# Fused attention, mixture of experts and gated layer: experts in two groups of four, and a fixed table of operations in place of the planner

## The chip, the cores and the metric

The kernel runs on one core of a Trainium2 chip. The metric is the device time of one execution in microseconds (us); lower is better. Three runs of the kernel before gave 447.46, 447.50 and 449.27 us, median 447.5.

## What is computed

Three layers follow one another on 1536 tokens (batch 2, 768 positions) of width 512. First, attention with 8 heads of 64, in which every query and every key is given to the nearest of 16 centroids of its head, and a query sees only keys of the same centroid. Second, a soft mixture of 8 experts with 4 slots each:

```python
logits = x @ phi                                   # 1536 x 32
d = softmax of logits over the tokens; c = softmax of logits over the slots
slot_input = (d.T @ x).reshape(8, 4, 512)
for e in range(8):
    h = np.maximum(slot_input[e] @ w1[e], 0.0)     # 4 x 1024
    slot_out[e] = h @ w2[e]                        # 4 x 512
x = c @ slot_out
```

Third, a root-mean-square norm and `(silu(xn @ w_gate) * (xn @ w_val)) @ w_out`, with 1536 inner columns. All arrays are float32.

## The kernel before, in words

**Attention.** The heads are taken in eight pairs. `prepare(i)` loads and transposes pair i (`turn`, `keep`), splits queries and keys in a high and a low part (`head`, `rest`), scores them against the centroids (`cluster`), makes one-hot rows (`argmax`, `onehot`, `ok`, `oq`) and moves parts with SyncE DMAs. Each pair has two units (halves of the queries). `unit(u)` computes scores once for the row maxima (`s1`, line 617, and `s1max` on VectorE, line 629), again with keys on the partitions (`s2`, lines 697 and 699), exponentiates on ScalarE (`exp`, line 706), multiplies with the values (`av`, line 723), and sums the six exponentials of the unit (`acc`, line 305, five additions of 128x768). The PSUM ring `big` has three buffers for `turn`, `s1`, `s2` and `lT`.

**Experts.** The slot inputs (`SITz`) are ready some 8 us after attention's last matmul. The 64 weight tiles of 512 KB (w1 and w2, 32 each) are loaded in the order in which the loop of `tile_kernel` at line 1997 lists them, the first 40 while attention runs, the rest as buffers come free. Experts go in four pairs. For a pair, `h1` (line 1454) accumulates over four parts of the width, with two experts times two halves of the 1024 inner columns in the four 32-row strips of one bank; then `relu`, four transposes (`hT`, line 1468), a copy (`hTe`), four `h2` (line 1480), a copy (`h2e`), and `cols` (line 1495, 8 matmul records), which adds the two halves with the matrix `F8` and writes the slot outputs by columns; `socs` and `gcols` copy them with and without the norm's gain. `warm` operations are matmuls without use that fill TensorE's waits; W1, W2, W3 and W9 are their numbers in the last pair.

**Gates.** `gram` and `cq` give the norm from the slot outputs, `x2`, `rms` and `scale` finish it, `part` and `cT` put the scaled slot weights in place, `gp` and `put` multiply the slot outputs with the gate and value weights. After that TensorE does 72 `mm` (line 1810) and 144 `om` (line 1848, three matmuls each) until the end. Weights of the last layer are decoded on ScalarE and VectorE (`mag`, `bits`) and split by `hi` and `lo`; `lo` and some of the `hl` run on GpSimd (line 305).

**Order.** Each operation is a closure with the engines that may run it, estimated durations, a key, and what it depends on; `Sched.op` collects some 1,900 of them, numbered from 0 in order of creation. `Sched.run` (line 201) plans them at build time: it takes again and again the ready operation and engine with the earliest start after penalties (keys with the offsets KO by name and SHIFT by number) and emits it. The order of emission is the order on each engine; waits between engines are semaphores that the framework adds.

Of the kernel before, what the change touches and what calls it, by code (L numbers as in the profile page):

```python
# [27 lines left out]
def bc(ap, n):  # L28
# [23 lines left out]
W9 = 8  # L52
# [4 lines left out]
W1 = 16  # L57
W2 = 8
W3 = 9
# [27 lines left out]
KO = {  # L87
    "acc": 1106.61, "argmax": 340.28, "av": 1317.56, "bits": 77.89, "both": -631.52, "cT": -252.33, "cTe": 2148.93,
    "centroids_": -906.44, "cevac": -692.62, "cluster": 703.68, "clusterT": -435.04, "cols": -526.12,
    "cq": -1953.73, "csm": -1921.26, "dexp": 1823.66, "drec": -318.51, "ds": -3013.83, "dsum": 256.8, "dz": 1821.6,  # L90
    "exp": 552.16, "fes": -661.41, "fexp": -316.11, "fold": -1112.56, "four": -693.77, "fsi": 2185.37,
    "fz": -548.31, "gcols": -2661.57, "gh": 2566.76, "gp": -1829.04, "gpk": 615.23, "gram": -328.99, "h1": -2309.88,
    "h2": 1318.49, "h2e": -2012.01, "hT": -343.76, "hTe": -479.39, "head": 3947.79, "hf": -705.62, "hh": -47.09,
    "hi": -212.93, "high": -1707.34, "hl": 524.04, "keep": 2847.0, "lT": 3.15, "lga": -820.49, "lgm": 934.58,
    "lgt": 814.78, "lgx": -617.39, "lgx0": -2320.67, "linv": -192.64, "lo": 333.83, "load": -352.41,
    "low": -2417.19, "lsum": 2484.96, "mag": 1056.41, "mb": 1281.87, "mbe": 155.41, "mm": 857.14, "mp": 4.41,
    "mp1": -354.58, "mpT": 217.04, "mrow": -453.01, "mv": -459.26, "mx": 1177.33, "nmT": -1237.86, "nrow": 431.94,
    "oT": -1122.62, "od": 1854.19, "oe": -269.77, "ok": -155.6, "om": 1947.6, "onehot": -2302.02, "oq": 996.66,
    "osb": 2866.99, "part": 1651.97, "pre": -2523.99, "put": -52.28, "put4": 2025.22, "qhi": -32.32, "qlo": 2773.53,
    "raw": -660.15, "ready": -508.02, "relu": -165.55, "rest": -573.48, "rms": 1037.95, "root": -316.14,  # L100
    "rowmm": 460.36, "rowput": -750.84, "s1": -1.39, "s1max": -454.29, "s2": 0.21, "scale": 1161.73, "sel": -868.48,
    "setup": 363.79, "si": 91.62, "siT": -250.83, "siT0": 277.65, "siTe": 414.23, "side": 336.02, "sie": 105.19,
    "silu": 2.05, "siz": -1847.17, "socs": 527.72, "square": -516.11, "sums": 484.54, "to_out": 2146.21,
    "to_tail": 3598.45, "to_wp": -1357.1, "to_wv": -909.45, "to_wx": -442.15, "to_wy": 771.46, "to_wz": 3452.96,
    "trans": -76.76, "turn": -5.08, "warm": 109.11, "wload": 2775.16, "x2": -540.95, "xrow": 1179.62,
}


# [5 lines left out]
class Op:  # L114
    __slots__ = ("eng", "fn", "deps", "key", "alloc", "uses", "end", "users", "left", "next", "ready", "seen", "after", "then", "lock")

    def __init__(self, eng, fn, deps, key, alloc, uses):
        self.eng, self.fn, self.key = eng, fn, key
        self.deps, self.alloc, self.uses = deps, alloc, uses
        self.end = None  # L120
        self.users = {}
        self.next = []
        self.after, self.then = (), []
        self.lock = False


SHIFT = {
# [31 lines left out]
}  # L159


class Sched:

    LAT = dict(pe=180, act=140, dve=100, pool=80)  # L170

    HALF = ("av", "cluster", "rowmm")
    TO, FRO, COLD = 85, 130, 75

    SAME = 30

    TAIL = 130

    def __init__(self, rings):
        self.rings = rings  # L180
        self.given = {t: [] for t in rings}
        self.ops = []
        self.slack = {}

    def op(self, eng, fn, deps=(), key=0.0, alloc=(), uses=(), after=(), lock=False):


        o = Op(eng, fn, [d for d in deps if d is not None],
               round(key + KO.get(opname(fn), 0) + SHIFT.get(len(self.ops), 0), 3), alloc, uses)
        o.after = [d for d in after if d is not None]  # L190
        o.lock = lock
        for t in alloc:
            o.users[t] = [o]
        for a, t in uses:
            a.users[t].append(o)
            if a is not o and a not in o.after:
                o.deps.append(a)
        self.ops.append(o)
        return o

    def run(self):
        free = {}
        for o in self.ops:
            o.left = len(o.deps) + len(o.after)
            o.ready = 0.0
            for d in o.after:
                d.then.append(o)
            for d in o.deps:
                d.next.append(o)
# [4 lines left out]
        def more(o, e, st):  # L214
            if e != "pe" or o.key > 99:
                return 0
# [1875 lines left out]
```

## Time and profile before

| What | Value |
|---|---|
| Median of three runs | 447.5 us |
| The profiled execution's own time, its span | 449.08 us, 447.4 us |
| TensorE matmul busy | 435.1 us (97%), 2798 matmuls |
| VectorE, ScalarE, GpSimd busy | 304.8, 241.7, 212.8 us |
| Mean granted TensorE clock | 0.996 of full speed |
| HBM read | 61.97 MB |

TensorE is busy from end to end. Matmul ends are modelled, so short waits are seen better in the distance of starts and in the chain of waits than in the busy share. In the 40 slices of the page the DMA engines are at nine tenths or more from slice 24 to slice 27, which is the stage of the experts.

### The profile page before, as it was taken

What the parts mean: (1) busy time and instruction counts of PE and PEld (TensorE: products, weight loads), DVE (VectorE), ACT (ScalarE), POOL (GpSimd) and SP (SyncE); (2) the same over time, 40 slices, a digit from 0 to 9 for tenths busy, and PEclk for the clock granted to TensorE, in tenths of its full rate; (3) what the DMA queues carried; (4) which work ended last, traced back from release to release, by engine and by line L of the source; (5) the groups of instructions that cost most, each with busy time, mean ns of one, the idle gap of its engine ahead of it and who ended that gap; (6) DMA issues with size and microseconds to landing.
All of it is one profiled execution on the core that took longest, in us unless ns stands there. A gap on an engine that the chain in (4) does not pass through costs nothing.

```text
span 447.4 us, 7789 instructions
## 1 busy us (share of the span) xinstructions
PE 435.1 (97%) x2798; PEld 309.7 (69%) x2798; DVE 304.8 (68%) x576; ACT 241.7 (54%) x448; POOL 212.8 (48%) x152
## 2 busy tenths in 40 slices
PE   7898999999999999999999999999999999999998
PEld 6675666676766766766767674356687778767887
DVE  6983878779857768676786762023978769986652
ACT  5266666577793873765734413134776684457430
POOL 1048857787885887666867210011440143125320
PEclk9999899999999999999999999999999999999999
DMA  6988799888575644546727489997125634510222
GB/s 198 231 226 241 191 252 273 254 235 223 143 208 161 164 129 89 131 134 191 212 89 301 180 311 397 390 400 289 40 94 190 234 96 142 188 47 1 94 96 94
DMA packets 32346, 84.54 MB, mean 189 GB/s; under 512 B 5082, under 2 KB 11316, under 8 KB 32308
## 3 DMA queue, kind: packets, MB, share of 16 engines
q1 hardware_dynamic: 30580, 77.76, 56.2%
q10 hardware_dynamic: 1728, 6.29, 4.6%
q8 instruction: 22, 0.36, 0.3%
q14 instruction: 16, 0.13, 0.1%
HBM read 61.97 MB, written 3.15 MB: 146 GB/s over the span
## 4 chain that ended last, share of the span: by engine, by line
PE 84%; DVE 4%; ACT 4%; issue 4%; POOL 2%; DMA 1%; ACTq 0%; POOLq 0%; DVEq 0%
PE o L1848 22%; PE o L723 14%; PE s L697 7%; PE s L617 7%; PE s L699 7%; PE h L1454 3%; PE h L1480 2%; PE pl L757 2%; PE g L1810 2%; PE v L1810 2%; ACT P L706 2%; PE pl L764 2%; DVE nm L629 2%; DMA rawq<-in_q_dram 1%; ACT k L549 1%
## 5 line engine op out<-in xcount | busy, mean ns | idle before, releaser
L305 POOL TENSOR_TENSOR acc<-acc,P 128x768 f32<-128x768 f32 x60 | 110.8, 1847 | 14.3 <-ACT P L706 10.3
L629 DVE TENSOR_REDUCE nm<-s 128x1 f32<-128x768 f32 x96 | 88.1, 953 | 30.8 <-PE s L617 30.1
L706 ACT ACTIVATE P<-s 128x768 f32<-128x768 f32 x96 | 74.1, 811 | 47.0 <-PE s L699 40.9
L1848 PE MATMUL o<-W,hh 128*128 128x512 f32 x288 | 89.3, 391 | 0.0
L697 PE MATMUL s<-q,k 128*128 128x384 f32 x192 | 68.5, 357 | 1.2 <-DVE kxq L299 0.5
L723 PE MATMUL o<-P,rawv 128*64 128x384 f32 x384 | 68.6, 494 | 0.0
L699 PE MATMUL s<-q,k 97*128 97x384 f32 x192 | 64.9, 338 | 0.0
L1848 PEld LDWEIGHTS o<-W,hh 128*128 128x128 f32 x288 | 53.7, 188 | 13.3 <-issue 2.4
L1848 PE MATMUL o<-W,hl 128*128 128x512 f32 x144 | 56.1, 390 | 0.0
L617 PE MATMUL s<-k,q 96*128 96x384 f32 x192 | 51.5, 370 | 4.3 <-DVE nm L629 2.1
L723 PEld LDWEIGHTS o<-P,rawv 128*64 128x64 f32 x384 | 24.9, 136 | 30.9 <-issue 29.7
L617 PEld LDWEIGHTS s<-k,q 96*128 96x128 f32 x192 | 31.4, 191 | 17.7 <-DVE nm L629 6.8
L697 PEld LDWEIGHTS s<-q,k 128*128 128x128 f32 x192 | 36.4, 189 | 9.1 <-issue 3.0
L305 POOL TENSOR_TENSOR acc<-P,P 128x768 f32<-128x768 f32 x15 | 27.4, 1830 | 27.2 <-ACT P L706 27.1
L305 POOL TENSOR_TENSOR W<-wo,W 128x512 fp32r<-128x512 f32 x12 | 16.3, 1363 | 50.4 <-ACT W L297 47.9
L699 PEld LDWEIGHTS s<-q,k 97*128 97x128 f32 x192 | 36.5, 190 | 0.0
L305 POOL TENSOR_TENSOR hl<-hf,hh 128x512 fp32r<-128x512 f32 x14 | 18.8, 1349 | 27.7 <-ACT hh L297 17.3
L1848 PEld LDWEIGHTS o<-W,hl 128*128 128x128 f32 x144 | 27.0, 188 | 5.7
L1822 DVE TENSOR_TENSOR hf<-v,sg 128x512 f32<-128x512 f32 x36 | 24.4, 689 | 9.2 <-POOL hl L305 5.3
L1818 ACT ACTIVATE sg<-g 128x512 f32<-128x512 f32 x36 | 21.2, 600 | 15.7 <-DVE hf L1822 12.6
L297 ACT CAST hh<-hf 128x512 fp32r<-128x512 f32 x30 | 18.7, 622 | 19.1 <-PE o L1848 15.4
L305 POOL TENSOR_TENSOR lok<-kxk,hik 128x768 fp32r<-128x768 f32 x7 | 12.8, 1826 | 27.7 <-ACT hik L297 21.6
(290 smaller groups left out, 690.8 us busy)
## 6 DMA issues: line engine op xcount, KB each, us to landing
w<-in_moe_w_dram SPq DMA_DIRECT2D x56, 512.0 KB, 5.4
k<-hik SPq DMA_DIRECT2D x32, 192.0 KB, 3.2
out<-in_moe_w_out_dram SPq DMA_DIRECT2D x12, 512.0 KB, 5.1
q<-hiq SPq DMA_DIRECT2D x28, 192.0 KB, 2.8
gate<-in_moe_w_gate_dram SPq DMA_DIRECT2D x8, 512.0 KB, 4.4
val<-in_moe_w_val_dram SPq DMA_DIRECT2D x8, 512.0 KB
rawk<-in_k_dram SPq DMA_DIRECT2D x8, 384.0 KB
rawq<-in_q_dram SPq DMA_DIRECT2D x8, 384.0 KB
```

The source lines that it names most:

```text
L297: nc.scalar.copy(out, in_)
L305: (nc.vector if e == "dve" else nc.gpsimd).tensor_tensor(out, a, b, op=op)
L617: nc.tensor.matmul(ps[:, g, :HQ], T[q2][0:96, h, qb : qb + 128], T[f"k2_{i}_{g}"][0:96, h, :], start=True, stop=True,)
L629: nc.vector.tensor_reduce(T[f"nm{u}"][:, n : n + 1], T[f"s1_{u}{h}{j}"][:, :, :HQ], op=ALU.max, axis=AX.XY, negate=True)
L697: nc.tensor.matmul(ps[:, h, :HQ], T[f"k1_{i}_{g}"][:, h, kb], T[q1][:, h, :], start=True, stop=False)
L699: nc.tensor.matmul(ps[:, h, :HQ], T[f"k2_{i}_{g}"][0:97, h, kb], T[q2][0:97, h, :], start=False, stop=True)
L706: nc.scalar.activation(p, T[f"s2_{u}_{c}"][:, :, :HQ], AF.Exp, scale=float(1.0 / D**0.5))
L723: nc.tensor.matmul(T[f"o{u}"][64 * h : 64 * h + 64, :HQ], T[f"rawv{i}"][:, h, c % 3 * 2 + c // 3, :], T[f"P{u}_{c}"][:, h, :], start=(c == ...
L1810: nc.tensor.matmul(self.bank(f"{which}{tg}_{f}", "pa"), T["Gst"][:, (FF if which == "v" else 0) + f * 128 :][:, :128], self.cc(1, tg, 1), ...
L1818: nc.scalar.activation(self.tile(f"sg{tg}_{f}", [128, 512], F32, "sg", "outp", 2), T[f"g{tg}_{f}"], AF.Silu)
L1822: nc.vector.tensor_tensor(self.tile(f"hf{tg}_{f}", [128, 512], F32, "hf", "outp", 2), T[f"v{tg}_{f}"], T[f"sg{tg}_{f}"], op=ALU.mult)
L1848: nc.tensor.matmul(T[f"o{k}{tg}{q}"], T[f"{x}{tg}_{f}"][:, ts], Wf(f)[:, w], start=(f % 4 == 0 and n == 0), stop=(f % 4 == 3 and n == 2))
```

## The change

1. **Experts in two groups of four.** The four strips of a bank now hold four experts, and the two halves f of the inner columns have banks of their own for `h1`. `h2` accumulates both halves in one bank over eight steps, so nothing is left to add: `cols` and what follows it run once for a group, and `F8` becomes `F16`, a copy. The matmuls of `h1` and `h2` stay 64 and 64, the transposes 16. Weights are loaded by group.
2. **Fill matmuls** of the last stage: W1 from 16 in four places to 6 in two, W2 from 8 in four to 4 in four, W3 from 9 to 8.
3. **The planner is gone.** `ORDER` lists all 1884 operations by number and `ENGINE` names the engine where there is a choice. The first 74 entries are those that the planner of before emits. Operations 0 to 1229 have the numbers of before; 1230 to 1289 are the experts (1230-1237 the eight `h1` of the first group, 1244-1251 its `h2`, 1253 its `cols`; 1256-1259, 1261, 1262, 1264, 1265 the `h1` of the second, 1272-1283 its `h2` with fills between, 1286 its `cols`); from 1290 on they are the numbers of before less 10. Compared name by name with the planner's order, 18 more of the 79 `acc` run on VectorE (22 in place of 4: four of unit 14, three of unit 0, two each of units 2, 10 and 11, one each of five others), with 2 `lsum`, 4 `head` and 4 `keep`; 5 `xrow` go from VectorE to ScalarE; five `lo` and some `hh` go to VectorE. `onehot` of pair 1 stands between the two `av` of unit 0 where it stood behind both, and `lo` of part 1 stands behind the `part` operations of the gates where it stood ahead of them.
4. `cq` of the second part has a bank of its own.

```diff
-W1 = 16
-W2 = 8
-W3 = 9
+W1 = 6
+W2 = 4
+W3 = 8
+ORDER = """
+0 8 11 9 1 10 2 148 3-4 12 24 7 13-14 5 15 26 6 25 27 146 16 36 28-29 38 18 37 17 39 19 40-41 30 42 31 43-44 20 45
...
+1163-1171 1085 1087-1090 1096 1107 1092-1095 1086 1091 1101 1099 1102 1097 1100 1108 1098 1104-1106 1230-1237 1109
+1238-1239 1242 1256 1240 1244-1247 1241 1257 1243 1248-1249 1172-1206 1250 1258-1259 1251 1261 1103 1262 1110 1252
...
     def run(self):
-        free = {}
...
+        for at, k in enumerate(order):
+            o = self.ops[k]
+            e = next(iter(o.eng)) if len(o.eng) == 1 else self.LETTER[next(engines)]
...
             o.fn(e)
...
-            def h1(dc, ep=ep, es=es):
+            def h1(dc, f, g=g, es=es):
...
+                        nc.tensor.matmul(
+                            T[f"h1{g}{f}"][32 * x : 32 * x + 32, :], T["SITz"][:, dc, ex, :],
+                            W.T["w1", ex, dc][:, f * 512 : (f + 1) * 512],
+                            start=(dc == 0), stop=(dc == 3),
+                        )
...
+                        nc.tensor.matmul(
+                            T[f"h2{g}"][32 * x : 32 * x + 32, :],
+                            T[f"hTs{g}{f}"][:, c * 128 + 32 * x : c * 128 + 32 * x + 32],
+                            W.T["w2", ex, 2 * f + c // 2][:, (c % 2) * 512 : (c % 2) * 512 + 512],
+                            start=(fc == 0), stop=(fc == 7),
+                        )
...
+                self.bank(f"cq{k}", "pb" if k else "pc")
...
-        for ep in range(NE // 2):
-            es = (2 * ep, 2 * ep + 1)
+        for es in (range(4), range(4, 8)):
             order += [("w1", e, dc) for dc in range(4) for e in es]
-            order += [("w2", e, 2 * f + kk) for kk in range(2) for e in es for f in range(2)]
+            order += [("w2", e, n) for n in range(4) for e in es]
```

## Rows read from the trace of the kernel before

**Rows 1.** Busy time by stretch: us, busy PE, PEld, DVE, ACT, POOL, clock, DMA share, GB/s.
```profile
100.00:140.00 40.00, 38.13 (x230) 25.99 (x226) 31.10 (x49) 28.14 (x60) 32.29 (x23) 1.00 0.72 203
...
290.00:300.00 10.00, 10.00 (x100) 4.81 (x96) 1.80 (x6) 2.54 (x6) 0.58 (x1) 1.00 1.03 401
```
**Rows 2.** Chain of waits through the experts: start, us, what.
```profile
270.09 7.07 PE h L1454 x64
...
283.36 1.04 PE sc L1495 x8
...
295.15 0.68 PE hT L1468 x4
295.82 0.89 PE warm141.4_3449 L1126 x16
...
297.24 3.57 PE h L1480 x32
```
**Rows 3.** Timeline of the experts: start, us, engine, line, operation [idle before].
```profile
277.95 0.69 DVE L299 COPY hTs<-hT 128x512 f32<-128x512 f32 x1 [6.39 <-PE hT L1468]
...
302.88 3.64 PE L1480 MATMUL h<-w,hTs 128*32 128x512 f32 x32
...
306.72 0.58 ACT L297 COPY H2s<-h 128x512 f32<-128x512 f32 x1 [3.15 <-PE h L1480]
...
308.84 1.08 PE L1556 MATMUL gram<-SOc 128*128 128x32 f32 x8
```
**Rows 4.** Weight DMAs of the experts: the last issues, and the times to landing.
```profile
289.58 9.30 SPq L1050 DMA_DIRECT2D w<-in_moe_w_dram  x8
...
DMA to landing us min/median/max: 3.5/4.5/7.0
```
**Rows 5.** Timeline of the gates: start, us, engine, line, operation [idle before].
```profile
314.05 1.29 POOL L305 TENSOR_TENSOR W<-wo,W 128x512 fp32r<-128x512 f32 x1 [1.07 <-ACT W L297]
314.12 1.24 DVE L1612 TENSOR_TENSOR srt<-srt,ms 128x4 f32<-128x4 f32 x1
...
314.47 1.28 ACT L1655 ACT_TABLE_LOAD   x1
...
315.20 0.59 PE L1674 MATMUL gpg<-wga,SOg 128*64 128x512 f32 x1
...
316.08 0.16 DVE L1612 TENSOR_TENSOR srt<-srt,ms 128x8 f32<-128x8 f32 x1
...
316.20 0.23 DVE L299 CAST cc<-Cx 128x128 fp32r<-128x128 f32 x1
...
318.01 0.69 DVE L1706 TENSOR_TENSOR Gst<-gpv,Gh 64x512 fp32r<-64x512 f32 x1
...
319.13 0.48 PE L1810 MATMUL g<-cc,Gst 128*128 128x512 f32 x1
```
**Rows 6.** Timeline of pairs 0 to 2, from 36 to 43 us.
```profile
36.43 5.83 POOL L305 TENSOR_TENSOR acc<-acc,P 128x768 f32<-128x768 f32 x3
...
38.67 1.90 DVE L299 CAST hik<-kxk 128x768 fp32r<-128x768 f32 x1 [4.83 <-DMA q<-hiq]
...
41.49 0.44 PE L697 MATMUL s<-q,k 128*128 128x384 f32 x1 [0.51 <-DVE kxq L299]
...
43.02 3.05 PE L617 MATMUL s<-k,q 96*128 96x384 f32 x8 [0.56 <-ACT P L706]
```
**Rows 7.** Busy time of a stretch behind them, columns as in rows 1.
```profile
43.98:47.40 3.42, 3.42 (x14) 1.37 (x13) 3.31 (x4) 1.63 (x3) 3.34 (x3) 0.50 0.78 160
```
**Rows 8.** Groups in attention: line, operation, count, busy us, mean ns, idle before.
```profile
L305 DVE TENSOR_TENSOR acc<-acc,P 128x768 f32<-128x768 f32 x3 | 2.9, 958 | 1.4 <-ACT P L706 1.2
...
L299 DVE CAST xd<-kxq 128x768 fp32r<-128x768 f32 x1 | 0.6, 561 | 0.0
...
L305 POOL TENSOR_TENSOR acc<-acc,P 128x768 f32<-128x768 f32 x60 | 110.8, 1847 | 14.3 <-ACT P L706 10.3
```
**Rows 9.** Who waited for whom before TensorE's weight loads in attention: us, times, longest.
```profile
PEld s L617 <- DVE nm L629: 6.8, 10, 1.2
PEld s L617 <- ACT P L706: 6.6, 15, 0.9
```

More of the change, by code (lines that the diff above doesn't have):

```diff
@@ L84 @@
 LK, LS = 0.61, 0.72
[L87 to L106, printed above, removed]
 def opname(fn):
@@ L114 @@
 class Op:
-    __slots__ = ("eng", "fn", "deps", "key", "alloc", "uses", "end", "users", "left", "next", "ready", "seen", "after", "then", "lock")
+    __slots__ = ("eng", "fn", "deps", "alloc", "uses", "users", "after", "at", "key")
     def __init__(self, eng, fn, deps, key, alloc, uses):
-        self.eng, self.fn, self.key = eng, fn, key
-        self.deps, self.alloc, self.uses = deps, alloc, uses
-        self.end = None
+        self.eng, self.fn, self.deps, self.key, self.alloc, self.uses = eng, fn, deps, key, alloc, uses
@@ L201, in run @@
     def run(self):
-        free = {}
[L203 to L209, printed above, removed]
-        avail = [o for o in self.ops if not o.left]
-        done = 0
-        half = False
-        def more(o, e, st):
-            if e != "pe" or o.key > 99:
-                return 0
-            h = opname(o.fn) in self.HALF
-            return (self.TO if h else self.FRO) if h != half else 0 if h or st < free.get(e, 0.0) + 5 else self.COLD
@@ L286, in run @@
-        assert done == len(self.ops), "ops left over"
-        return max(o.end for o in self.ops)
+        order = []
+        for w in ORDER.split():
+            a, _, b = w.partition("-")
+            order += range(int(a), int(b or a) + 1)
+        assert sorted(order) == list(range(len(self.ops))), "an op is missing or there twice"
+        engines = iter("".join(ENGINE.split()))
+        given = {t: [] for t in self.rings}
+        for at, k in enumerate(order):
+            o = self.ops[k]
+            e = next(iter(o.eng)) if len(o.eng) == 1 else self.LETTER[next(engines)]
+            assert e in o.eng
+            assert all(d.at is not None for d in o.deps + o.after), "an op comes ahead of what it needs"
+            for t in o.alloc:
+                n = len(given[t]) - self.rings[t]
+                assert n < 0 or all(x.at is not None for x in given[t][n].users[t]), "a buffer is still in use"
+                given[t].append(o)
+            o.fn(e)
+            o.at = at
@@ L1441, in experts @@
         self.sog = []
-        self.soc, two = [], [[], []]
-        for ep in range(NE // 2):
-            es = (2 * ep, 2 * ep + 1)
-            kk = k0 + 10 * ep
-            def h1(dc, ep=ep, es=es):
+        self.soc = []
+        for g in range(2):
+            es = range(4 * g, 4 * g + 4)
+            kk = k0 + 20 * g
+            def h1(dc, f, g=g, es=es):
                 def fn(e):
                     if dc == 0:
-                        self.bank(f"h1{ep}", "pb")
+                        self.bank(f"h1{g}{f}", "pb")
@@ L1464, in hT @@
-            def hT(e, ep=ep):
-                ps = self.bank(f"hT{ep}", "pa")
-                for c in range(4):
-                    x = T[f"H1s{ep}"].rearrange("p (n x c) -> p n c x", n=2, c=2)
-                    nc.tensor.transpose(ps[:, c * 128 : (c + 1) * 128], x[:, c // 2, c % 2], K["id"])
-            def hTe(e, ep=ep):
-                copy(nc, e, self.tile(f"hTs{ep}", [128, 512], F32, "Hs"), T[f"hT{ep}"])
-            def h2(fc, ep=ep, es=es):
+                        nc.tensor.matmul(
[3 more added lines that the diff above has]
+                        )
@@ new lines, in h1, with relu, hT, fn @@
+                return fn
+            def relu(f, g=g):
+                return lambda e: nc.scalar.activation(self.tile(f"H1s{g}{f}", [128, 512], F32, "Hs"), T[f"h1{g}{f}"], AF.Relu)
+            def hT(f, g=g):
+                def fn(e):
+                    ps = self.bank(f"hT{g}{f}", "pa")
+                    x = T[f"H1s{g}{f}"].rearrange("p (n x c) -> p n c x", n=2, c=2)
+                    for c in range(4):
+                        nc.tensor.transpose(ps[:, c * 128 : (c + 1) * 128], x[:, c // 2, c % 2], K["id"])
+                return fn
@@ L1474, in fn, with hTe, h2 @@
+            def hTe(f, g=g):
+                return lambda e: copy(nc, e, self.tile(f"hTs{g}{f}", [128, 512], F32, "Hs"), T[f"hT{g}{f}"])
+            def h2(fc, g=g, es=es):
+                f, c = divmod(fc, 4)
                 def fn(e):
                     if fc == 0:
[L1476 removed]
+                        self.bank(f"h2{g}", "pb")
                     for x, ex in enumerate(es):
[L1478 to L1485 removed]
@@ L1486, in h2 @@
-                return fn
-            def h2e(e, ep=ep):
-                copy(nc, e, self.tile(f"H2s{ep}", [128, 512], F32, "Hs"), T[f"h2{ep}"])
-            def cols(e, ep=ep):
-                ps = self.bank(f"sc{ep}", "pa")
+                        nc.tensor.matmul(
[4 more added lines that the diff above has]
+                        )
@@ L1494, in cols, with h2e @@
+                return fn
+            def h2e(e, g=g):
+                copy(nc, e, self.tile(f"H2s{g}", [128, 512], F32, "Hs"), T[f"h2{g}"])
+            def cols(e, g=g):
+                ps = self.bank(f"sc{g}", "pa")
                 for c in range(4):
-                    nc.tensor.matmul(ps[:, 64 * c : 64 * c + 64].rearrange("p (r n) -> p r n", n=8), T[f"H2s{ep}"][:, c * 128 : (c + 1) * 128],
-                                     T["F8"].rearrange("p x s -> p (x s)").unsqueeze(1).to_broadcast([128, 8, 8]),
-                                     start=True, stop=True)
@@ L1521, in experts @@
-            b = op({"pe": 440}, hT, key=kk + 2.2, alloc=("pa",), uses=[(a, "Hs")])
-            a = op({"act": 480, "dve": 600}, hTe, key=kk + 2.3, alloc=("Hs",), uses=[(b, "pa")])
-            gs = []
-            for fc in range(4):
-                if ep == 3:
-                    self.warm(W2, gs[-1:] or [a], kk + 3.9 + 0.5 * fc)
-                x2 = [W.half.get(("w2", ex, 2 * f + fc // 2)) for ex in es for f in range(2)]
-                gs.append(op({"pe": (860, 900)}, h2(fc), deps=x2 if fc % 2 else [], after=gs[:1] + gs[-1:], key=kk + 4 + 0.5 * fc,
+                if g and dc > 1:
+                    self.warm(W1, hs[-1:], kk + 0.5 * dc - 0.1)
@@ new lines, in experts @@
+                for f in range(2):
+                    hs.append(op({"pe": (860, 900)}, h1(dc, f), deps=[self.slots], after=hs[-1:], key=kk + 0.5 * dc + 0.2 * f,
+                                 alloc=("pb",) if dc == 0 else (),
+                                 uses=[W.O["w1", ex, dc] for ex in es] + ([(hs[f], "pb")] if dc else [])))
+            ts = []
+            for f in range(2):
+                a = op({"act": 600}, relu(f), deps=[hs[f - 2]], key=kk + 2.1 + 0.05 * f, alloc=("Hs",), uses=[(hs[f], "pb")])
+                b = op({"pe": 440}, hT(f), key=kk + 2.2 + 0.05 * f, alloc=("pa",), uses=[(a, "Hs")])
+                ts.append(b)
@@ new lines, in experts @@
+            hts = [op({"act": 600, "dve": 690}, hTe(f), key=kk + 2.3 + 0.05 * f, alloc=("Hs",), uses=[(ts[f], "pa")]) for f in range(2)]
+            gs = []
+            for fc in range(8):
+                if g and fc > 3:
+                    self.warm(W2, gs[-1:], kk + 3.9 + 0.5 * fc)
+                f, c = divmod(fc, 4)
+                x2 = [W.half.get(("w2", ex, 2 * f + c // 2)) for ex in es]
+                gs.append(op({"pe": (860, 900)}, h2(fc), deps=x2 if c % 2 else [], after=gs[-1:], key=kk + 4 + 0.5 * fc,
```

245 lines of the change are left out of this document (106 added, 139 removed), and 31 rows, old and new, of the table SHIFT.

## The prediction

> **What bounds the kernel now.** I read the page's busy shares first, then the busy time by stretch, then the chain of waits. In every stretch TensorE is the wall: 38.1 of 40 us at 100 to 140 us, 10.0 of 10 in the experts [rows 1]. The chain of waits stays on TensorE through the experts, one block behind the other: eight `h1` in 7.07 us, four `h2` in 3.57 [rows 2]. So time goes only where TensorE gets less to do, or where one of its waits ends sooner. The timeline of a stretch shows the second kind: behind the experts TensorE waits for a chain of small operations [rows 5], and at 41 to 43 us for a bank and a buffer [rows 6]. In the experts the DMA engines are full as well, a share of 1.03 and 401 GB/s [rows 1]: they are the second wall there, and it stands close.
>
> The profiled execution took 449.08 us with a span of 447.4, so 1.7 lie around the span. It holds one thing that I don't expect in each execution: from 43.98 to 47.40 us the granted clock was 0.50, the lower of its two levels (1.2 for 2.4 GHz) [rows 7], behind two waits of TensorE of 0.5 us each [rows 6]. Half of 3.42 is 1.7 us. The other timed runs, 447.46 and 447.50, lie 1.6 below 449.08, as if they had no such fall. So I take 449.08 - 1.7 = 447.4 as the execution without it, which is the median, and don't count the fall as a gain.
>
> **The change, part by part.**
>
> *Experts: matmuls.* One `h1` or `h2` is four matmuls in four strips, 3.57 / 4 = 0.89 us [rows 2]; there are 32 of them on either side. Transposes are 16 on either side. `cols` costs 1.04 us [rows 2]; three of four lay between the `h1` and `h2`, now one of two does: 2 x 1.04 = 2.1 us less. Fills ahead of the last `h2`: 10 + 16 before, by the table 5 + 6 + 12 now, at 0.89 / 16 = 56 ns [rows 2]: 0.2 less. TensorE is full here, so both are on the path: -2.3.
>
> *Experts: the end.* Behind the last `h2` come a copy, `cols`, `socs` and `gram`, from 306.45 to 308.84 us [rows 3]. The copy goes to VectorE: 0.69 for 0.58 [rows 3], +0.1; `socs` copies 256 columns in place of 128, which no row shows: from 0 to the 0.69 of a 512-column copy; I take +0.1, since the whole copy of 512 columns costs only 0.69. Fills there lie in the wait.
>
> *Experts: waits and loads.* With one group the `h2` of the first half must wait for `relu`, `hT` and `hTe`, some 0.6 + 0.7 + 0.7 us (as the copies and the transposes of rows 2 and 3). The table puts one `h1` of the second group (0.89) and, for the other half, four `h2` (3.57) beside them. From 0 to 0.5 us may stay open; I take 0.1. Loads: 24 of the 64 tiles are left behind the first 40 on either side, and the buffers of the first group's w1 come free as early as before; those of the last four tiles wait for the sixth `h2`, by my count at 270.1 + 16 x 0.89 + 2 x 0.68 = 285.7 us [rows 2], ahead of the first of the last eight issues at 289.6 [rows 4]. The last half tile was issued at 298.6; with the shortest landing, 3.5 us [rows 4], it is there at 302.1, and it was there at 305.5, when the last of four `h2` of 302.88 to 306.45 began [rows 3]. In the new order the `h2` that needs it starts at 306.45 - 2.3 - 0.9 = 303.3. So this costs from 0 (landing at 302.1) to 2.2 us (305.5). Nearer rows than the two ends there are none; since the shares before are full and the seven other halves were issued earlier, I take 0, and keep the 2.2. Experts in sum: -2.3 + 0.2 + 0.1 = -2.0.
>
> *Gates.* A multiplication of 4 columns took 1.24 us at 314.12 where the same line took 0.16 at 316.08 [rows 5]; it ended when GpSimd's `lo` (314.05 to 315.34) ended. That `lo` is moved behind `part`. What is late next: `part` on VectorE comes 1.08 earlier, at 315.1; then the three `put` on VectorE, which need `gp`, whose last matmul ends at 315.8 [rows 5] and 0.2 earlier with four fills for eight ahead of it. The first `put` then starts at 315.65 for 316.38, and the third ends at 317.8 for 318.70 [rows 5]. On ScalarE the table load until 315.75 [rows 5] keeps its `part` at 315.96 for 316.20, which the `put` don't need. First `mm` at 318.2 for 319.13: -0.9. If ScalarE's copies are late, half of it is lost (-0.45). The moved `lo` is wanted by the second `om` block, some 4 us later, behind one `hl` on GpSimd: nothing, or up to 1.3 (its own length) if it is late. The bank for the second `cq` takes a slot that is free then: 0.
>
> *Pairs 0 to 2.* A cast on VectorE took 1.90 us at 38.67 [rows 6] against 0.56 for this shape [rows 8], beside GpSimd's three `acc` [rows 6]. The copy behind it was late, and TensorE waited 0.51 and 0.56 us [rows 6]. In the table GpSimd has three `acc` less here, and `onehot` of pair 1 comes one `av` earlier, so ScalarE's `ok` and `oq` lie beside that `av`. VectorE gets three `acc` (3 x 0.96) and a `rest` (0.96) ahead of the copies, while TensorE has some 6 us of `av` and `turn`. Between 0 and -1.1; I take -0.8.
>
> *The rest of attention.* 15 more `acc` move from 1.85 us on GpSimd to 0.96 on VectorE [rows 8], and many neighbours change places. No row shows that order. From below, the waits of `s1` for VectorE and ScalarE, 6.8 + 6.6 us [rows 9], could go by half: -6.7. From above: rival 2, +6.7. VectorE's share is 31.1 of 40 [rows 1], and every unit must have its six maxima, so I see no reason for either sign: 0. The last layer (the same 72 `mm` and 144 `om`) is costed at 0 as well, from -1 to +1 by the same token.
>
> The Trainium skill, Perfetto Trace Analysis, Optimizing Scalar/DVE Operations, says that GpSimd and VectorE share a read port, so that moving work between the two may not help. This case's rows agree that they block one another (1.24 and 1.90 us above). By that rule alone the -0.8 of the pairs would be 0 and the sum -2.9.
>
> Sum: -2.0 - 0.9 - 0.8 = -3.7. Against 449.08 this is 445.4 with the fall of the clock and 443.7 without it; against the median of the runs, 447.5, it is **443.8 us**.
>
> **Rivals.**
> 1. *The weights are the wall.* The last half tile lands when the last `h2` began before, at 305.5: of the -2.0 nothing is left, and -0.9 - 0.8 gives 445.8. For it: the full DMA share. Against it: the queue had issued the last tile seven us earlier.
> 2. *Slower: VectorE makes TensorE wait.* A moved `acc` that stands ahead of a row maximum for which `s1` waits keeps a bank 0.96 us longer. It decides once VectorE has no idle time left in a unit. If seven of the 14 moved outside unit 14 do so, 7 x 0.96 = 6.7, and the time is 443.8 + 6.7 = 450.5. For it: TensorE already waits for these maxima, 6.8 us [rows 9]. Against: VectorE idles 8.9 of 40 us [rows 1], and the move makes a sum shorter by half.
> 3. *The new order of attention is better everywhere.* A quarter of the waits of rows 9, 13.4 us, goes as well: 443.8 - 3.4 = 440.4. Nothing in the profile speaks for it but that there are waits.
> 4. *The clock falls.* With 38 fills for 58 between `gram` and the first `om`, the granted clock drops there as it did at 44 us: +1.7, 445.5. Against it: it was 1.00 in both stretches of rows 1.
>
> **How the numbers follow.** Forecast 0.50 (own range 441.5 to 446.0), rival 1 0.15, rival 2 0.12, rival 3 0.17, rival 4 0.06. A measurement of this kernel tells some 0.5% (2.2 us) from no change: faster means below 445.3. Of the forecast 0.43 lies there, of rival 1 0.04, of rival 4 0.02, all of rival 3: 0.66. Slower, above 449.7: rival 2, 0.12. The rest, 0.22, is no change. The range 439.5 to 448.0 leaves out most of rival 2 and a part of rival 3.
>
> **What would show it.** In the changed trace: two `cols` blocks of 1 us; `gram` some 2 us earlier after the first `h1` than 308.84 - 270.09 = 38.8 us; no `h2` that starts behind a DMA; the multiplication at line 1612 at 0.16 us and `gram` to first `mm` 0.9 shorter than 10.3 us; no wait of 0.5 us of `s1` and `s2` for pair 2. Attention's length, first `h1` at 270.1, tells rivals 2 and 3: above 273 is the one, below 267 the other. A first `h1` that moves by more than the 0.8 would make the prediction wrong, whatever the experts do.

## The result, and the profile after

The changed kernel takes 453.1 us (median of 20 runs, 448.5 to 458.1); the kernel before, timed beside it, 448.7 us (20 runs, 447.3 to 452.4). The ratio is 1.0065, 95% interval 1.0036 to 1.0094: slower by some 0.7%. It leaves out, as slow, six of the changed kernel's 20 runs that lie over 1.5% above its fastest, all at a mean clock below 0.99; the medians, which hold all runs, differ by 1.0%. The forecast was 443.8 us, 439.5 to 448.0, faster. The profiled execution took 452.78 us, with a span of 451.1; all rows of the changed kernel are from it.

Where its time went, by the moments that the prediction named, each minus the same moment of the kernel before: first `h1` +1.3 us (271.37 for 270.09), `gram` +0.5 (309.39 for 308.84 [rows 3]), first `mm` +2.2 (321.32 for 319.13 [rows 5]), first `om` +2.1 (324.70 for 322.59), last `om` +3.7 (446.99 for 443.31). So attention lost 1.3, the experts gained 0.7, the gates lost 1.6 and the last layer lost another 1.6.

*The clock.* Two stretches of the changed kernel; the columns are those of rows 1 (busy us and count of each engine, granted clock, DMA share, GB/s).

```profile
300.00:312.10 12.10, 11.58 (x109) 6.32 (x101) 5.76 (x15) 4.94 (x9) 2.38 (x4) 1.00 0.86 320
312.10:318.93 6.83, 6.83 (x24) 2.73 (x23) 2.88 (x15) 2.09 (x5) 1.58 (x5) 0.50 0.10 39
```

In the gates the granted clock is 0.50, 1.2 in place of 2.4 GHz, for 6.83 us; the kernel before had its one low stretch at 44 us [rows 7]. This differs from execution to execution: at a mean clock of 0.999 and more the changed kernel's span was 447.2 and 447.6 us, at 0.985 it was 454.4 to 456.3. The mean over its 20 executions is 0.991; over 120 of the kernel before, timed beside the experiments, 0.995.

*The experts' end and the gates.* Timeline of the changed kernel, answering to rows 3 and 5:

```profile
307.15 0.61 PE L1060 MATMUL warm<-idb 128*128 128x128 bf16 x8
307.76 1.10 PE L1427 MATMUL sc<-F,H2s 128*128 128x64 f32 x8
309.39 1.08 PE L1489 MATMUL gram<-SOc 128*128 128x32 f32 x8 [0.52 <-DVE SOc L233]
...
314.56 0.16 DVE L1544 TENSOR_TENSOR srt<-srt,ms 128x4 f32<-128x4 f32 x1
...
318.53 0.79 PE L1604 MATMUL gpv<-wga,SOg 128*64 128x512 f32 x1
...
321.32 0.50 PE L1740 MATMUL g<-cc,Gst 128*128 128x512 f32 x1 [0.21 <-ACT cc L231]
```

The multiplication of 4 columns that took 1.24 us [rows 5] takes 0.16, as forecast. But now TensorE idles 0.52 us between `cols` (`sc`) and `gram`, where the kernel before had nine fills; and at half clock the last `gp` begins at 318.5, so that the first `mm` starts 11.93 us behind `gram` for 10.29. The fills of the kernel before:

```profile
308.30 0.67 PE L1126 MATMUL warm<-idb 128*128 128x128 bf16 x9
```

*The experts.* Pieces of the chain of waits (start, us, what), answering to rows 2:

```profile
279.12 1.00 PE h L1385 x8
280.12 3.43 PE h L1413 x32
283.55 0.68 PE hT L1400 x4
284.23 1.00 PE h L1385 x8
...
296.08 0.69 PE hT L1400 x4
296.77 0.03 issue
296.80 0.02 DVEq L233
296.82 0.04 issue
296.86 0.70 DVE hTs L233
297.56 0.04 issue
297.61 4.50 PE h L1413 x40
```

Eight `h` matmuls that stand alone take 1.00 us; inside a long block eight take 0.86 (3.43 / 4). In the second group the copy `hTs` is on the chain with 0.70 us (0.84 from `hT` to the next `h2`): nothing is left to lay beside it.

*Attention.* Timeline of the changed kernel at pairs 0 to 3, answering to rows 6; in brackets is the idle time ahead and what ended it. `kxk` and `kxq` are the transposed keys and queries of a pair, `hik`, `hiq`, `lok` and `loq` their high and low parts (one buffer for `hi`, one for `lo`), `nr` the row maxima, which a transfer writes into `q`:

```profile
34.17 0.27 PE L608 MATMUL pm<-idr,nm 128*6 128x128 f32 x1 [0.96 <-DVE E L453]
...
41.48 0.34 PE L633 MATMUL s<-q,k 97*128 97x384 f32 x1
...
43.07 1.03 PE L551 MATMUL s<-k,q 96*128 96x384 f32 x4
...
58.04 0.83 ACT L231 CAST hiq<-kxq 128x768 fp32r<-128x768 f32 x1 [2.86 <-DMA k<-lok]
...
60.18 0.44 PE L631 MATMUL s<-q,k 128*128 128x384 f32 x1 [1.58 <-ACT kxk L231]
...
91.20 0.83 ACT L231 CAST hiq<-kxq 128x768 fp32r<-128x768 f32 x1 [3.50 <-POOL L L239]
91.94 2.21 ACT L640 ACTIVATE P<-s 128x768 f32<-128x768 f32 x3
...
92.80 0.62 PE L551 MATMUL s<-k,q 96*128 96x384 f32 x2 [1.00 <-ACT P L640]
```

The two waits of rows 6 are gone (no bracket from 41 to 43 us). Three others are there: 0.96, 1.58 and 1.00 us. Two of them have a `hiq` cast in front: it waits 2.86 and 3.50 us at the head of ScalarE's queue, and the copy `kxk` and the exponentials `P` behind it wait with it.

*The last layer.* The 288 `om` matmuls on `hh`, in the kernel before and then in the changed one; the three numbers are least, median and longest ns of one. These views, here and below, are of 322 to 447 us, so the first or the last matmul can be missing from their count:

```profile
L1848 PE MATMUL o<-W,hh x288: 389/389/504, 322.6 to 443.1; 128*128 128x512 f32 x144
```

```profile
L1778 PE MATMUL o<-W,hh x288: 389/395/504, 324.7 to 446.8; 128*128 128x512 f32 x144
```

The same instruction takes 6 ns longer. From start to start it is 227 ns in the kernel before; in the changed one 231 to 235 on `W0` and `W2`, and 227 on `W1`.

### The profile page after: what moved, and what is told of

Same layout as the page of the kernel before. It is cut to its first block, busy times and chain, and to the rows that moved or that the text cites. A ratio compares the mean times of both kernels' runs of the same rounds, so it can differ in the third digit from the quotient of the medians.

```text
span 451.1 us, 7540 instructions
## 1 busy us (share of the span) xinstructions
PE 433.7 (96%) x2713; PEld 304.5 (68%) x2713; DVE 318.9 (71%) x619; ACT 223.6 (50%) x420; POOL 170.6 (38%) x129
## 4 chain that ended last, share of the span: by engine, by line
PE 80%; DVE 5%; ACT 5%; issue 4%; DMA 3%; SPq 1%; POOL 1%; ACTq 0%; DVEq 0%; POOLq 0%
PE o L1778 22%; PE o L657 12%; PE s L631 7%; PE s L551 6%; PE s L633 6%; PE h L1385 3%; PE h L1413 3%; ACT P L640 2%; PE pl L691 2%; PE pl L698 2%; PE v L1740 2%; PE g L1740 2%; DMA k<-hik 2%; DMA q<-nr 1%; DVE nm L563 1%
## 5 line engine op out<-in xcount | busy, mean ns | idle before, releaser
L239 POOL TENSOR_TENSOR acc<-acc,P 128x768 f32<-128x768 f32 x45 | 83.6, 1858 | 44.8 <-DVE acc L239 32.4
L1778 PE MATMUL o<-W,hh 128*128 128x512 f32 x288 | 90.7, 396 | 0.0
L239 POOL TENSOR_TENSOR hl<-hf,hh 128x512 fp32r<-128x512 f32 x15 | 19.9, 1326 | 75.7 <-ACT hh L231 59.4
L483 ACT ACTIVATE k<-pe,ebias,escale 33x384 fp32r<-33x384 bf16 x30 | 18.1, 662 | 20.5 <-PE pe L468 16.3
L239 POOL TENSOR_TENSOR acc<-P,P 128x768 f32<-128x768 f32 x12 | 21.9, 1826 | 13.7 <-ACT P L640 13.6
L231 ACT CAST hh<-hf 128x512 fp32r<-128x512 f32 x23 | 14.2, 620 | 16.6 <-DVE hf L1752 12.9
```

Source lines behind the costliest of these rows:

```text
L239: (nc.vector if e == "dve" else nc.gpsimd).tensor_tensor(out, a, b, op=op)
L483: nc.scalar.activation(T[f"k2_{i}_{g}"][64:97, h], pe(g)[:33], AF.Identity, bias=bias, scale=scale)
L1778: nc.tensor.matmul(T[f"o{k}{tg}{q}"], T[f"{x}{tg}_{f}"][:, ts], Wf(f)[:, w], start=(f % 4 == 0 and n == 0), stop=(f % 4 == 3 and n == 2))
```

## Experiments

In the tables an operation is a number; "order" diffs show the operation that moves. "Full clock" means executions with a mean granted clock of 0.998 and more.

**1 and 2. Attention exchanged.**

```
-ORDER, ENGINE: all operations ahead of the first h1 as changed
+ORDER, ENGINE: the same operations in the order, and on the engines, of the kernel before
```

The second is the other way round: the kernel before, with all that is ahead of the first `h1` as changed.

> The changed kernel with every operation ahead of the first h1 in the order and on the engine that the kernel before had; experts, gates and last layer as changed. Theory A (attention's new order costs 3.0 us: the first h1 came at 271.4 us for 270.1, and the 270.1 holds a clock fall of 1.7 us): executions without a clock fall go from 448.6 to about 445.6 us, first h1 near 268.4 without a fall. Theory B (the rest of the loss is clock falls for want of fills in the gates): the falls stay, the granted clock is 0.985 to 0.995 in most executions and the median is about 450. Rival C (the falls come from attention's order): clock 0.996 or more in most executions, median about 446. If the order costs nothing, the median stays at 453.

> The kernel before from the first h1 on, with the changed kernel's order and engines ahead of it. Theory A: executions without a fall at 447.4 + 3.0 = 450.4 us, first h1 near 271.4. Theory B: clock mostly 0.996 or more, as in the kernel before, median 450.4 to 451.5. Rival C: the falls come along, clock 0.985 to 0.995, median 453 to 454. If attention's order costs nothing, 448.7 as before.

The first: median 449.9 us (12 runs), ratio 0.9995 (0.9962 to 1.0028); full-clock spans 445.0 to 446.8, first `h1` 269.65, mean clock 0.993. The second: median 453.0 (12 runs), ratio 1.0031 (0.9993 to 1.0069); full-clock spans 446.0 to 450.1, mean clock 0.995. By the first, theory A holds in sign: its interval lies below that of the changed kernel. The second alone can't be told from no loss, and its one profile has a first `h1` of 269.58, no loss at all; so the size is uncertain. In the first, `gram` to first `mm` took 8.73 us and first to last `om` 122.25: the gates' gain and the last layer's loss are there without the new attention.

**3 and 4. More fills.**

```
-W1, W2, W3 = 6, 4, 8
+W1, W2, W3 = 16, 8, 9
...
-WG = (16, 6, 4, 0, 0)
+WG = (32, 6, 4, 0, 0)
-    self.warm(W2, gs[-1:], kk + 3.9 + 0.5 * fc)
+    self.warm(W2 if fc < 7 else 8, gs[-1:], kk + 3.9 + 0.5 * fc)
```

> The changed kernel with the fill counts of the kernel before (16, 8, 9 for 6, 4, 8). On the path: 10 + 3 x 4 = 22 more fills ahead of the last h2 at 56 ns, +1.2 us. Theory B (falls for want of fills in experts and gates): clock 0.996 or more in most executions, median 453.1 - 3 + 1.2 = about 451. Otherwise the falls stay and the median is 454.3.

> The changed kernel with 20 more fills behind gram (16 more behind the last gp, 4 more between two gp), so 48 for 28; some 1.1 us of fills, mostly beside the wait for the gates, 0 to +0.9 on the path. Theory B: full clock from gram to the first mm, gram to first mm about 9 us for 11.9; most executions at 0.996 or more, median 449.5 to 450.5. If the falls don't come from this want of fills: the low stretch at 312 stays or turns up elsewhere, median 453 to 454.

The first: 453.4 us (11 runs), ratio 1.0076 (1.0044 to 1.0107), mean clock 0.994; `gram` came 39.64 us behind the first `h1` for 38.02, so the fills cost 1.6. The second: 454.0 us (12 runs), ratio 1.0088 (1.0052 to 1.0125), mean clock 0.992, and its profile has the same fall, at 311.81. More fills behind the first `gp` don't hold the clock: theory B falls in the form "too few fills in the gates".

**5 and 6. The place of one tile.** `F16` of the changed kernel is 64 bytes a partition, `F8` of the kernel before 32. Tiles that are opened later lie lower by the difference, `W0`/`W2` among them.

```
-self.tile("F16", [128, 16], F32).rearrange(
+self.tile("F16", [128, 24], F32)[:, :16].rearrange(
...
-self.tile("F8", [128, 2, NS], F32),
+self.tile("F8", [128, 4, NS], F32)[:, :2],
```

> The changed kernel with the tile F16 made 96 bytes a partition (24 columns, 16 used) for 64, so that the tile W0/W2 of the output weights starts 32 bytes lower: at byte 194592 of a partition for 194624 (194656 in the kernel before). Theory E (in the last layer an om matmul starts 231 to 235 ns behind the one ahead in place of 227 because the moving operand W0/W2 lies 32 bytes off, as the fold tile grew from 32 to 64 bytes; W1, whose place is the same in both kernels, runs at 227): the pitch is 227 ns again in all of the last layer, first om to last om 120.7 us for 122.3, the median lower by some 1.5 us (451.5 for 453). Rival F (the last layer is longer because of the order of its matmuls): pitch and length stay, 122.3.

> The kernel before with its tile F8 made 64 bytes a partition (half of it unused) for 32, which puts W0/W2 at byte 194624, where the changed kernel has them. Theory E: the pitch of om on W0 and W2 rises to 231 to 235 ns, first om to last om from 120.7 to 122.2 us, median 450 to 451. Rival F: nothing changes, 120.7 us.

The second settles that the place is the cause; its group, after those shown above:

```profile
L1848 PE MATMUL o<-W,hh x287: 387/395/504, 324.7 to 446.8; 128*128 128x512 f32 x144
```

In the kernel before, with nothing changed but an unused half of a small tile, `om` takes 395 ns for 389, and first to last `om` 122.6 us for 120.7. Median 452.6 (10 runs), ratio 1.0040 (1.0007 to 1.0072). The first was a miss: 32 bytes further down it stays slow (median 393 ns, 122.3 us; 451.4 us, 10 runs, ratio 1.0035, 0.9998 to 1.0072). So the place counts, but not by its remainder modulo 64, which is 32 at 194656 (fast) and at 194592 (slow). Other tiles moved along with `W0` and `W2`; that `om` on `W1`, which keeps its place, stays at 227 ns from start to start in both runs speaks for the place of the `W` tile itself.

**7. One transfer moved.**

```
-ORDER ... 283 132 136 125 196 232 197-198 284 ...
+ORDER ... 283 284 132 136 125 196 232 197-198 ...
```

> The changed kernel with one operation moved: the second k<-lok transfer of pair 2 stands ahead of the q<-nr transfer on SP's queue, not behind it. Theory G (SP's queue holds that transfer 3 to 4 us for q<-nr, so ScalarE's hiq cast and the copy kxk behind it come late and TensorE waits up to 1.6 us at 58 us): the wait of TensorE at 58 us goes (1.58 us in the changed kernel's trace, 0 to 1.8 in the others with its order), median lower by 0 to 1.5 us. Rival H (the landing itself is slow, whatever its place in the queue): the wait stays in the same range.

The wait at 58 us is gone (`hiq` waits 0.8 us for 2.9), but TensorE waits 1.03 us at 90.2 and 1.09 at 93.5. 454.6 us (7 runs), ratio 1.0085 (1.0041 to 1.0128). G holds for the one wait; in the time nothing of it can be seen.

**8. Fills between `cols` and `gram`.**

```
-ORDER ... 1286 1292 1288 ... 1414 1394 1287 1396 ...
+ORDER ... 1286 1287 1292 1288 ... 1414 1394 1396 ...
...
+    self.warm(W2 if fc < 7 else 8, gs[-1:], kk + 3.9 + 0.5 * fc)
```

> The changed kernel with its 8 fills W9 put between the last cols and gram, where TensorE idles 0.5 us, in place of behind the transposes of the gates, and 8 for 4 fills between two gp. Theory B2 (the clock falls at 312 us because of the idle time between cols and gram): no low stretch at 312; mean granted clock over the executions from 0.991 to 0.995 or more, median 451. If the fall at 312 has another cause: the mean clock stays at 0.991 to 0.993, median 453.

Its timeline, and the stretch that was at half clock:

```profile
306.45 1.10 PE L1426 MATMUL sc<-F,H2s 128*128 128x64 f32 x8
307.39 0.61 PE L1059 MATMUL warm139.17_3600<-idb 128*128 128x128 bf16 x8
308.07 1.08 PE L1488 MATMUL gram<-SOc 128*128 128x32 f32 x8
...
317.02 0.49 PE L1739 MATMUL g<-cc,Gst 128*128 128x512 f32 x1 [0.68 <-ACT cc L230]
```

```profile
312.00:319.00 7.00, 6.22 (x51) 3.34 (x47) 5.55 (x21) 5.09 (x11) 2.37 (x7) 1.00 0.00 1
```

Median 450.2 us (12 runs) for 453.1, ratio 1.0006 (0.9972 to 1.0039), mean clock 0.997 for 0.991, and `gram` to first `mm` 8.95 us for 11.93. The four extra fills are also in experiment 4, where the fall stayed; what differs is that eight fills left their place further back for the 0.52 us in front of `gram`. Of nine profiles without fills there, three have a low stretch that begins between 311.8 and 314.4; of the five with them, none. That is too few to decide, but the executions agree: with attention as changed, 17 of 31 without these fills (the changed kernel, experiments 5 and 9) have a mean clock of 0.992 or less, and 4 of 24 with them (8 and 12).

**9 and 10. Another place; six operations of attention put back.**

```
-self.tile("F16", [128, 16], F32).rearrange(
+self.tile("F16", [128, 40], F32)[:, :16].rearrange(
...
-ORDER: 161, 278, 284, 293, 294, 404 at 107, 205, 214, 255, 313, 334
+ORDER: 161, 278, 284, 293, 294, 404 at 111, 153, 202, 238, 272, 302
```

> The changed kernel with the tile F16 made 160 bytes a partition (16 of 40 columns used), which puts W0/W2 at byte 194528. The two slow places so far are 194624 and 194592, the fast ones 194656 (W0/W2 of the kernel before) and 62304 (W1); the stationary operand hh lies at 136800 and up by 2048. Modulo 128 the fast places and hh all leave 96, the slow ones 64 and 32; 194528 leaves 96. Theory E2 (the pitch is 227 ns where the moving tile's place leaves the same remainder modulo 128 as the stationary's): pitch 227 ns in all of the last layer, first om to last om 120.7 us for 122.3. Rival E3 (only the very place, or a coarser remainder, counts: modulo 256 it leaves 224 for 96): pitch 231 to 235 ns on W0 and W2, 122.3 us.

> The changed kernel with six operations of attention put back to where the kernel before has them: the hiq cast of pair 1 behind the argmax chain, the GpSimd subtractions lok of pairs 2 and 3, one k<-lok transfer of pair 2 and two q<-loq transfers. Theory G2 (in the new table GpSimd's lok of pairs 2 and 3 comes 7 to 8 us later, 49.7 for 43.0 and 82.4 for 74.0 us; ScalarE's hiq cast, behind it in the chain, then stands 0.7 to 3.0 and 2.3 to 4.7 us at the head of ScalarE's queue with kxk and the exp activations behind it, and TensorE waits for these): no idle of more than 0.5 us ahead of hiq at pairs 2 and 3, no wait of TensorE at 32.9, 58 and 89 to 95 us (in sum 2 to 3.7 us in the traces with the new order); first h1 at 268.5 to 269.5 us without a clock fall ahead of it, median 451 to 452 for 453. Rival V (VectorE, with 18 acc more, is what TensorE waits for): these waits come back as waits for VectorE's nm, first h1 stays at 270 to 271.

The place 194528 is slow too (392 ns, 122.1 us; one run): modulo 128 is refuted. The six operations: 452.7 us (11 runs), ratio 1.0047 (1.0012 to 1.0083). At pair 2 `hiq` waits 0.29 us and TensorE's waits at 33 and 58 us are gone; at pair 3 it still waits:

```profile
91.48 0.84 ACT L230 CAST hiq<-kxq 128x768 fp32r<-128x768 f32 x1 [2.96 <-DMA k<-hik]
```

The two `k<-hik` transfers stand behind a `q<-nr` on SP's queue (issued at 85.0 and 85.6 us; 82.2 and 82.8 in experiment 1). There are waits of 0.75 us at 41.7 and 2.51 us at 136.7, both for `q<-nr`; the second, of 0.66 us and more, is in six other profiles with the new order of pair 4 as well. G2 names waits that go when these operations go back, but the ratio can't be told from the 1.0065 of the changed kernel.

**11, 12 and 14. Everything together, with three kinds of attention.** All have the fills of experiment 8 and `F16` padded to 288 bytes, which puts `W0`/`W2` at 194400.

```
-self.tile("F16", [128, 16], F32).rearrange(
+self.tile("F16", [128, 72], F32)[:, :16].rearrange(
...
11: ORDER, ENGINE ahead of the first h1 as in the kernel before
12: ORDER, ENGINE ahead of the first h1 as changed
14: the first 195 operations as changed, the rest of attention as before
```

> Attention in the order and on the engines of the kernel before; experts, gates and last layer as changed; the 8 fills W9 between cols and gram (8 for 4 between two gp), and the tile F16 padded to 288 bytes, which puts W0/W2 at byte 194400: modulo 256 that leaves 96, as 194656, 62304 and 136800 (hh) do. Theory E3 (what counts is the remainder modulo 256): om pitch 227 ns, first om to last om 120.7 us for 122.3; the slow places 194624, 194592 and 194528 leave 64, 32 and 224. If it is neither remainder: 231 to 235 ns, 122.3. The sum of the terms: full-clock span 446.1 - 0.4 (experts) - 1.5 (gates) = 444.2 for 446.1 of the kernel before, mean clock 0.996, median 446 to 447, a ratio of 0.994. With the slow pitch 1.6 more: no gain that can be measured.

> The same as the kernel with attention of before, fills and the padded tile, but with attention in the new order. The difference of the two is attention alone: theory A (its new order costs some 1.5 us at full clock, since waits of TensorE of 0.5 to 1.8 us at 33, 58 and 89 to 95 us take the place of those at 41 to 43): full-clock span 445.7, median 448. If the new order costs nothing: as the other, 444.2 and 446.5.

> As the kernel with attention of before, fills and the padded tile, but the first 195 operations (up to some 54 us: pairs 0 and 1 and the first row maxima of unit 2) in the changed kernel's order and on its engines. Theory P (the prediction's term: the waits at 41 to 43 us go and that is worth 0.8 us; what the new order loses comes behind 54 us): full-clock span 0.8 lower than with all of attention as before, 443.4. If the new start costs as much elsewhere (a wait of 0.5 to 1.2 us at 33 us): the same 444.2.

Experiment 11: **446.7 us** (6 runs), ratio 0.9910 (0.9879 to 0.9942): faster than both kernels. Its `om` and `hiq`:

```profile
L1779 PE MATMUL o<-W,hh x286: 387/389/504, 322.0 to 441.2; 128*128 128x512 f32 x143
```

```profile
87.33 0.50 ACT L232 COPY cs<-pc 128x384 f32<-128x384 f32 x1
87.70 0.85 ACT L232 CAST hiq<-kxq 128x768 fp32r<-128x768 f32 x1
```

`om` is back at 389 ns and 120.4 us from first to last; the three fast places, 194656, 62304 and 194400, and that of `hh` all leave 96 modulo 256, the three slow ones 64, 32 and 224. In attention as before, `hiq` waits for nothing at pairs 2 and 3 (at pairs 4 to 7 it waits 0.4 to 1.5 us). Experiment 12: 449.9 us (12 runs), ratio 0.9982 (0.9957 to 1.0008). The two differ in attention alone, so its new order costs 3.3 us (by the ratios and their intervals 3.2, give or take 1.8). Experiment 14: 448.2 us (12 runs), ratio 0.9960 (0.9937 to 0.9983): with the new first 195 operations it is 1.5 us slower than 11. Theory P's gain is not seen, but it is not refuted either: where the two orders meet, TensorE waits 1.12 us for `P` at 54.3 us, behind a ScalarE operation that waits 1.65 us for a gate weight, and neither 11 nor 12 has that wait.

**13. The 18 `acc` back on GpSimd.**

```
-ENGINE: acc of 18 slots v
+ENGINE: the same 18 g
```

> The changed kernel with the 18 acc that it moved from GpSimd to VectorE back on GpSimd, the order kept. Rival V (the prediction's rival 2: VectorE, with 18 acc more, makes TensorE wait): attention 1 to 2 us shorter, full-clock span 446 for 447.3, median 451.5. Theory G2 (waits at the head of the queues of ScalarE and SP, not VectorE's load): unchanged or slower, as GpSimd takes 1.85 us for 0.96 and its lok come later still: full-clock span 447.3 to 449, median 453 or more.

455.8 us (5 runs), ratio 1.0117 (1.0078 to 1.0156), for 453.1 and 1.0065 (1.0036 to 1.0094) of the changed kernel. Rival V, which wanted it 1.5 us faster, is refuted. That the 18 `acc` on VectorE help this order is likely but not clear, since the intervals overlap.

**15. The mirror of 14.**

```
the first 195 operations as before, the rest of attention as changed
```

> The mirror of the kernel whose first 195 operations are in the new order: those 195 in the order and on the engines of the kernel before, all that follows in attention in the new order; fills and the padded tile as in both. With attention all old at a median of 446.7, all new at 449.9 and only the first 195 new at 448.2 us: if the two losses add, the rest alone costs 1.7 and the median is 448.4. If the loss is in the first 195 operations only, 446.7. If it comes from the rest whatever the start is (hiq at the head of ScalarE's queue at 89 us, a wait of 0.9 to 1.9 us at 131): 449.5 or more.

448.7 us (12 runs), ratio 0.9976 (0.9944 to 1.0008): +2.0 over all of attention as before. 1.5 and 2.0 add up to about the 3.3 of both, but each is uncertain by some 2 us, and the 1.5 holds the wait at the seam.

## Why the prediction was wrong

**The step that failed: "The rest of attention: 0".** It also took -0.8 for pairs 0 to 2. Measured, attention costs +3.3 us (11 against 12), where the sum had -0.8. The -0.8 was read from two waits, and these did go. But the prediction counted the waits that leave and none that come, though the table moved `lok`, `hiq` and their transfers as well. GpSimd's `lok` came at 49.7 for 43.0 us and 82.4 for 74.0 (changed kernel for experiment 1). ScalarE's `hiq` then waits at the head of its queue in every profile wholly in the new order (0.3 to 3.0 us at pair 2, 1.9 to 4.7 at pair 3), and at neither pair in any of the four wholly in the old one. Which of these waits reach TensorE differs from execution to execution. TensorE's idle time from 30 to 260 us is the 230 us less its busy time; here the changed kernel, experiment 12 and experiment 11:

```profile
30.00:260.00 230.00, 222.90 (x1387) 158.18 (x1386) 175.18 (x316) 136.31 (x261) 133.15 (x86) 1.00 0.66 189
```

```profile
30.00:260.00 230.00, 224.75 (x1384) 159.98 (x1385) 176.06 (x315) 136.91 (x260) 132.35 (x85) 0.99 0.66 188
```

```profile
30.00:260.00 230.00, 224.91 (x1390) 158.49 (x1389) 166.32 (x291) 140.94 (x266) 168.07 (x105) 0.99 0.67 193
```

With the new order it was 4.2 to 8.3 us (eleven profiles, those of experiments 7, 10 and 13 among them), with the old 4.9 to 6.3 (four): on average 1.2 us more (0.7 without those three), and less even. The very pair that gives the 3.3 us differs by 0.2 only. Its two profiles are level at the end of unit 6 (last `av` at 131.6 and 131.5 us) and 2.1 us apart at the end of unit 7: in experiment 12 TensorE waits 1.85 us for `q<-nr`, and a stretch at half clock follows (its row is below). Behind `hiq`, which waits 2.89 us at pair 3 there, it waits for 0.3 us at most. So waits that come are shown, for several transfers and casts, but how they add up to 3.3 us stays open. The mean clock is not the reason: it was 0.995 in experiment 11 and 0.997 in 12.

**Rivals 2 and 3** can be read from who waited for whom at `s1` and `s2` (us, times, longest), 30 to 260 us, experiment 11 and then 12:

```profile
PEld s L552 <- ACT P L641: 6.7, 15, 1.0
PEld s L552 <- DVE nm L564: 6.2, 9, 1.2
...
PEld s L632 <- DVE nm L564: 1.8, 3, 0.6
```

```profile
PEld s L550 <- ACT P L639: 5.2, 13, 0.6
...
PEld s L630 <- DVE nm L562: 2.8, 6, 0.6
...
PEld s L550 <- DVE nm L562: 2.3, 5, 0.8
```

Rival 2 is the one that forecast slower, and its 450.5 is the nearest, but its mechanism is refuted: with the new order the weight loads wait less for VectorE's maxima (5.1 for 8.0 us), and experiment 13 shows no gain without the 18 `acc`. Rival 3 is answered as well: the two waits of rows 9 are 12.9 us in the old order and 7.5 in the new, more than its quarter less, and attention was no shorter. So waits of weight loads that leave need not shorten the path. The Trainium skill (Perfetto Trace Analysis, Optimizing Scalar/DVE Operations) warns that work moved between GpSimd and VectorE may win nothing. Experiment 13 can't tell whether the move of the 18 `acc` won anything.

**Rival 4, "the clock falls", was right in kind, wrong in cause and price.** It was given a chance of 0.06 and a price of 1.7 us. In the gates a fall cost 3.2 us (11.93 against 8.73 in experiments 5 and 9, the same gates at full clock). What the runs point to is the idle 0.52 us ahead of `gram`, which the prediction dismissed with "Fills there lie in the wait", and not the count of fills behind `gram`; but the same 0.52 us is there in experiments 5 and 9 without a fall, so it makes one likely, not sure. Over the executions the fills in that place gave 2.9 us (453.1 to 450.2; ratio 1.0065 to 1.0006). The other low stretches ahead of the last matmul show the same: each begins in a wait of TensorE of 0.5 to 2.6 us or up to 3.1 us behind it (not every such wait is followed by one). Experiments 10 and 12, behind waits of 2.51 and 1.8 us for `q<-nr`:

```profile
136.91:140.33 3.42, 3.42 (x12) 3.42 (x13) 0.96 (x1) 1.17 (x2) 2.21 (x3) 0.50 0.02 8
```

```profile
134.09:137.50 3.41, 3.41 (x12) 3.41 (x12) 0.96 (x1) 1.36 (x2) 2.69 (x4) 0.50 0.08 19
```

In the old order it is the waits at 41 to 43 us of rows 6 that such a stretch follows (at 44.0 in the kernel before, 45.1 in experiment 11); in experiment 14, which has no wait there, eight of twelve executions were at 1.000. So a wait of TensorE can be paid twice. The prediction did not expect that fall of the kernel before in each execution and left it out of both sides. Of 120 executions of the kernel before 35 were at 1.000 and 44 at 0.996, the value of the profile with its one stretch; these are 1.85 us longer (median span 447.95 for 446.1). So its 1.7 us was about right, but 447.5 is the time of an execution without a fall, and the median of 20 is 448.7: 1.2 us of the miss.

**Last layer: 0, from -1 to +1.** Measured +1.6 (122.29 for 120.72) and, in experiment 6, +1.9 by the place alone. Nothing in the order did that: with the place right, the changed order takes 120.4. The diff showed the 32 bytes; the prediction read the line and priced only the operation.

**Experts: -2.0.** Measured -0.7 (38.02 for 38.75). The two `cols` did go. Three terms were too small. The waits were +0.1 in the forecast, and the wait for `hTs` of the second group alone is 0.84 us. The `h` blocks cut into eights, at 1.00 for 0.86 us, had no term; on the chain all blocks take 28.85 us for 28.36. The fills ahead of the last `h2` take 1.62 us for 1.45, where 0.2 less was forecast. The end was right: from the last `h2` to `gram` 2.52 us for 2.39, with `gram` waiting 0.52 in it. Rival 1 did not come about: no `h2` of the changed kernel's profile waits for a transfer. But its 302.1 was no bound: the 3.5 us of rows 4 is of the transfers of another line, and the one of the last eight whose landing the trace tells took 9.6 us.

**Gates: -0.9.** Right in mechanism, and too small: at full clock 8.73 to 8.95 us for 10.29, so -1.3 to -1.6.

The sum with measured terms: 448.7 (before, timed beside it) + 3.3 + 1.6 - 0.7 - 1.3 = 451.6. The rest to 453.1 fits the clock in the gates, of which experiment 8 gave back 2.9; with attention's 3.3 uncertain by 1.8, the sum does not show it.

## What to carry to other kernels

A new order by hand or by table is not neutral where TensorE is nearly always busy: list, for each in-order queue, which operation now stands at the head waiting for a buffer or a transfer, and who is behind it; and price the order by exchanging that part alone, as one profile shows only one of several outcomes. Put fills where TensorE waits, ahead of the stretch that must run at full clock, not where there is room for them. When a small tile changes its size, compare the addresses of the large tiles behind it: a pad of 224 bytes was worth 1.8 us here (120.4 for 122.25). With that pad, the fills and the old attention the change wins 0.9%.

## What the runs showed of the hardware

The start address of a matmul's moving operand changes its time: 389 ns at 194656, 62304 and 194400, 392 to 395 at 194624, 194592 and 194528, with the stationary operand `hh` at 140896, 142944 and 144992, which leave 96 modulo 256 like the fast three. Whether 96 modulo 256 counts by itself or because the stationary operand has it was not tried.

A low stretch of the clock (0.50) cost some 1.85 us for 3.41 us in the kernel before (the executions above, the wait ahead of it included), and 3.2 us for 6.83 us in the gates. One pair of profiles can mislead: the kernel before, with its stretch at 44 us, has its first `h1` only 0.4 us behind that of experiment 1 (270.09 for 269.65), but experiment 1 has a wait of 1.17 us at 47.7 that the other lacks.
